# Attention and gated MLP on one core: bound on v from a sum of magnitudes on ScalarE, batch 0 scaled at its split, row-sum constants on ScalarE

## Chip, cores and metric

The kernel runs on one core of a Trainium2 chip. The metric is the device time of one execution in microseconds (us). Times of the kernel before: 1137.96 us median of three runs (1137.18 to 1144.3).

## What is computed

```python
q_d = q.reshape(B, H, Sd, factor, D).mean(axis=3)   # factor 4: 576 rows -> 144
...
out_d = sm_attn(q_d, k_d, v_d)                      # softmax attention on the means
out_up = np.repeat(out_d, factor, axis=2)
mask = np.abs(pos[:, None] - pos[None, :]) < factor # local attention: 3 neighbours each side
...
attn = attn / (np.sum(attn, axis=-1, keepdims=True) + 1e-09)
x = out_up + np.matmul(attn, v)                     # B, H, S, D = 8, 8, 576, 64 -> x is 4608 x 512
...
gate = 1.0 / (1.0 + np.exp(-(x @ w_gate)))          # 512 -> 1536
return (gate * (x @ w_val)) @ w_out                 # 1536 -> 512
```

The inputs are float32. q and k are drawn at 0.1 and then multiplied by about 6.25, w_gate by 2.946.

## The kernel before, in words

**Units and chunks.** Attention is cut into 32 units u, one for each pair of heads of a batch (four units per batch: batch b holds units 4b to 4b+3). The MLP runs over nine chunks c of 512 tokens, each in twelve pieces fc of 128 hidden columns: a gate product `pg`, a value product `pv`, and an output product `po` that adds up over fc in four PSUM banks. A large product is made of three float16 products of high and low halves, so x is split into two float16 halves (tile `xT`).

**The steps of a unit.** prep1 copies q into a block-diagonal tile (`qblk`, L438). s0 and s1 compute the local scores (`s`), add the mask (L466), take the row maximum (`mx`, L477), subtract it on GpSimd (L478) and take the exponential on ScalarE (L479). sm sums the rows (`sm`, L484), adds a tiny constant and multiplies by another (L485), takes the reciprocal (L486) and multiplies (L488). d0 and d1 do the same for the pooled scores (`sd`, maximum `mxd` L511, scaled on ScalarE L512, exponential `e` with its row sums `sme` L514); dn adds the constant (L521), takes the reciprocal (L522) and normalises into `ad` (L527 or L531). vd sums v over groups of four rows into `vdblk` (L383, L385). a0, a1 and at transpose the probabilities (`at`, `adt`) and copy them out of PSUM on ScalarE (L538), od multiplies with pooled v (`od`), and x multiplies with v (`x`), adds both (`xs`, L583 or L585) and splits the sum into `xT` (L591, L593).

**Scales.** Each batch needs a bound on |v| before its x can be scaled into float16. `vmax` (a DVE maximum of magnitudes over 128x640 for each unit, L152 into tile `vm`; four are joined at L302) gives pvb, svb = 2/pvb and sxb = 4096 svb (L305). Units 0 to 7 are "plain": v stays float32 and x is scaled by sxb while it is read out of PSUM (L567, L583). Later units scale v itself (`vsplit`, L156 and L157).

**Weights.** Each of 36 weight tiles is loaded twice: once for its maximum (`hmx`, L152), once for the conversion into float16 halves (ScalarE L205, DVE L206 to L208, ScalarE L214 and GpSimd L215; for w_out ScalarE L156 and DVE L157). This runs beside batches 0 and 1 and the first chunk.

**What sets the order.** A table T gives every step a place on one line of positions (a_* for batch 0, m_* for the others); the steps are written out in that order, and a scheduler of the library orders the instructions by it on the five in-order engines. Most v, qk, qkd and vd loads and all weight loads are issued on SP's queue. Short dummy products (`awake`) stand among batch 0's steps on TensorE. On PSUM, batch 0 uses the MLP's banks for pooled products, and all `att` tiles of the units rotate through two banks.

## Time and profile before

| | |
|---|---|
| median of the runs shown | 1137.96 us |
| profiled execution | 1139.3 us, of which the span is 1137.5 us |
| TensorE (PE) busy | 1097.7 us (96%) |
| VectorE (DVE) busy | 566.8 us (50%) |
| ScalarE (ACT) busy | 488.1 us (43%) |
| GpSimd (POOL) busy | 335.5 us (29%) |
| mean granted TensorE clock | 0.968 |

The table's shares are over the whole span. The page also cuts the span into 40 slices of 28.4 us, and the trace can be asked for any stretch, so that the opening (batches 0 and 1, the weight conversions and the first chunk) and the long rest are read apart.

### The profile page before, as it was taken

To read this page: it belongs to the slowest core of one execution; us is meant where nothing else is said; L and a number is where in the kernel's file an instruction comes from. 1 tells how busy PE (TensorE), PEld (TensorE's weight loads), DVE (VectorE), ACT (ScalarE), POOL (GpSimd) and SP (SyncE) were. 2 spreads that over 40 slices of the span, in tenths; PEclk is the share of its full clock that TensorE was granted. 3 is DMA by queue.
4 is the path that set the end of the run, shared out by engine and by line. 5 is a ranking of instruction groups with operands and counts; after the bars stand their busy time and mean duration, and the time that the engine had idled before them with its cause. 6 is when DMAs were issued, how large, how long until landed. Compare 5 with 4: busy or idle time off the path is not lost.

```text
span 1137.5 us, 16128 instructions
## 1 busy us (share of the span) xinstructions
PE 1097.7 (96%) x6319; PEld 603.6 (53%) x6319; DVE 566.8 (50%) x1048; ACT 488.1 (43%) x1112; POOL 335.5 (29%) x352
## 2 busy tenths in 40 slices
PE   7879879999999999999999999999999999999998
PEld 5854534555555555555555555555555554444443
DVE  7789989854445544444444444444444432122121
ACT  6635666533445444444445443544454332112112
POOL 6335646222223333333333332333243210000000
PEclk9758889999999999999999999999999999999999
DMA  9887766332213222132223121311121000000001
GB/s 361 330 311 258 252 210 216 118 100 86 70 47 131 60 65 70 59 111 74 69 69 106 61 65 56 119 59 54 48 94 36 1 1 37 1 1 37 1 1 37
DMA packets 31900, 110.33 MB, mean 97 GB/s; under 512 B 3536, under 2 KB 3664, under 8 KB 31824
## 3 DMA queue, kind: packets, MB, share of 16 engines
q1 hardware_dynamic: 31824, 109.30, 28.7%
q8 instruction: 50, 0.82, 0.3%
q14 instruction: 26, 0.21, 0.1%
HBM read 99.84 MB, written 9.44 MB: 96 GB/s over the span
## 4 chain that ended last, share of the span: by engine, by line
PE 86%; DVE 7%; DMA 2%; ACT 2%; issue 1%; POOL 1%; SPq 0%; DVEq 0%; ACTq 0%; POOLq 0%
PE po L394 24%; PE pg L394 23%; PE pv L394 23%; PE s L394 5%; PE x L394 3%; PE sd L394 3%; PE od L394 2%; PE at L546 1%; PE adt L556 1%; DVE wrg L207 1%; DMA v<-in_v_dram 1%; DVE vdblk L385 1%; DVE hmx L152 0%; DMA wo3c<-in_wo_dram 0%; DVE wrv L207 0%
## 5 line engine op out<-in xcount | busy, mean ns | idle before, releaser
L394 PE MATMUL pg<-xT,wg 128*128 128x512 f16 x1296 | 311.9, 383 | 6.7 <-ACT wg L214 3.5
L394 PE MATMUL pv<-xT,wv 128*128 128x512 f16 x1296 | 311.8, 381 | 0.1
L394 PE MATMUL po<-g,wo 128*128 128x512 f16 x1188 | 280.8, 379 | 0.0
L394 PEld LDWEIGHTS <-wg 128*128 128x128 f16 x1296 | 125.8, 99 | 152.0 <-issue 7.7
L394 PEld LDWEIGHTS <-wo 128*128 128x128 f16 x1296 | 124.7, 99 | 153.1 <-issue 8.2
L394 PEld LDWEIGHTS <-wv 128*128 128x128 f16 x1296 | 125.6, 99 | 141.0 <-issue 4.9
L627 DVE SCALAR_TENSOR_TENSOR tanh<-tanh,pv 128x512 f32<-128x512 f32 x108 | 73.8, 683 | 203.6 <-PE pv L394 199.3
L619 ACT ACTIVATE tanh<-pg,tsc 128x512 f32<-128x512 f32 (+7 forms) x192 | 87.0, 497 | 163.7 <-PE pg L394 163.7
L635 ACT ACTIVATE g<-tanh,gs 128x512 f16<-128x512 f32 x99 | 71.5, 723 | 149.6 <-DVE tanh L627 148.4
L636 DVE SCALAR_TENSOR_TENSOR g<-tanh,gs,g 128x512 f16<-128x512 f32 x99 | 88.6, 895 | 52.4 <-ACT g L635 51.9
L478 POOL TENSOR_TENSOR t<-t,mx 128x640 f32<-128x640 f32 x32 | 44.0, 1376 | 186.5 <-DVE mx L477 186.5
L394 PEld LDWEIGHTS s<-qk,qblk 128*128 128x128 f32 x600 | 77.9, 198 | 10.6 <-DVE hx L191 1.9
L394 PE MATMUL s<-qk,qblk 128*128 128x64 f32 x600 | 77.1, 279 | 2.6 <-DVE hx L191 1.4
L593 POOL TENSOR_TENSOR xT<-xs,xT 128x384 f16<-128x384 f32 (+7 forms) x58 | 53.1, 928 | 74.1 <-ACT xT L591 73.7
L488 POOL TENSOR_TENSOR t<-t,sm 128x640 f32<-128x640 f32 x28 | 36.8, 1316 | 96.0 <-DVE sm L486 94.6
L484 DVE TENSOR_REDUCE sm<-t 128x10 f32<-128x640 f32 x32 | 26.1, 817 | 66.1 <-ACT t L479 66.0
L156 ACT ACTIVATE vblk<-v,svb 64x640 f16<-64x640 f32 x48 | 39.7, 827 | 34.6 <-PE x L394 32.9
L466 DVE SCALAR_TENSOR_TENSOR t<-s,mk 128x384 f32<-128x384 f32 x64 | 31.0, 486 | 41.9 <-PE s L394 41.8
L438 ACT COPY qblk<-qk 64x580 f32<-64x580 f32 x60 | 40.5, 676 | 23.2 <-DMA qk<-in_qk_dram 19.5
L157 DVE SCALAR_TENSOR_TENSOR vblk<-v,svb,vblk 64x640 f16<-64x640 f32 x48 | 47.3, 985 | 3.2 <-ACT vblk L156 1.6
L512 ACT ACTIVATE mxd<-mxd 72x2 f32<-72x2 f32 x64 | 13.0, 203 | 83.5 <-DVE mxd L511 83.2
L383 POOL TENSOR_TENSOR qkd<-qkd 128x576 f32<-128x576 f32 x29 | 40.1, 1382 | 28.9 <-DMA qkd<-in_qkd_dram 28.5
(292 smaller groups left out, 1180.3 us busy)
## 6 DMA issues: line engine op xcount, KB each, us to landing
qk<-in_qk_dram SPq DMA_DIRECT2D x30, 610.0 KB, 3.8
qkd<-in_qkd_dram SPq DMA_DIRECT2D x29, 576.0 KB, 3.8
vd<-in_vd_dram SPq DMA_DIRECT2D x29, 384.0 KB, 3.5
v<-in_v_dram SPq DMA_DIRECT2D x32, 320.0 KB, 3.0
out_dram<-osb SPq DMA_DIRECT2D x16, 512.0 KB, 3.1
wo<-in_qk_dram SPq DMA_DIRECT2D x2, 610.0 KB, 10.5
wo<-in_qkd_dram SPq DMA_DIRECT2D x2, 576.0 KB, 9.3
out_dram<-osb SPq DMA_DIRECT2D x4, 256.0 KB, 2.3
```

Source lines behind the costliest of these rows:

```text
L156: nc.scalar.activation(hi, src, AF.Copy, scale=sc)
L157: nc.vector.scalar_tensor_tensor(out=lo, in0=src, scalar=sc, in1=hi, op0=ALU.mult, op1=ALU.subtract)
L383: nc.gpsimd.tensor_tensor(out=x[:, :, 0:2], in0=x[:, :, 0:2], in1=x[:, :, 2:4], op=ALU.add)
L394: nc.tensor.matmul(o, w[a], x[c], start=first and i == 0, stop=last and i == len(pairs) - 1)
L438: nc.scalar.copy(QB[ps, :, ps.start : ps.start + R], q_[ps])
L478: nc.gpsimd.tensor_tensor(out=t, in0=t, in1=mx.unsqueeze(2).to_broadcast([P, NBLK, WIN]), op=ALU.subtract)
L488: eng.tensor_tensor(out=t, in0=t, in1=sm.unsqueeze(2).to_broadcast([P, NBLK, WIN]), op=ALU.mult)
L593: eng.tensor_tensor(out=x[:, hp, 1, o : o + n], in0=src, in1=x[:, hp, 0, o : o + n], op=ALU.subtract)
L619: nc.scalar.activation(t[:, o : o + n], pt[:, o : o + n], AF.Tanh, scale=tsc[:, b, fc : fc + 1])
L627: nc.vector.scalar_tensor_tensor(out=t, in0=t, scalar=1.0, in1=pt, op0=ALU.add, op1=ALU.mult)
L635: nc.scalar.activation(g[:, 0], t, AF.Copy, scale=gs[:, fc : fc + 1])
L636: nc.vector.scalar_tensor_tensor(out=g[:, 1], in0=t, scalar=gs[:, fc : fc + 1], in1=g[:, 0], op0=ALU.mult, op1=ALU.subtract)
```

## The change

Four edits, and one number of the table T (batch 0's a_vd, the place of the pooled sums of v, goes from 1.97 to 4.6).

- `vmax` takes on ScalarE the sum of |v| over a partition's 640 values, with the accumulator of an Abs activation, in place of the DVE maximum. A sum of magnitudes is never below their maximum, so it bounds v too; the factor VUP = 512 goes into svb and out of sxb again.
- For units 0 to 3, x is read out of PSUM unscaled, and scaled by sxb in `split` (ScalarE activation with a scale, DVE multiply and subtract). Before, units 0 and 1 had their low half computed on GpSimd, units 2 and 3 on DVE; now all four have it on DVE.
- The constants of the row sums `sm` and `sme` (two tiny DVE operations for each unit) go to ScalarE.
- Batch 0's pooled sums of v are written at a later place.

```diff
-        absmax(vm[b][:, hp : hp + 1], vraw[u].rearrange("p a b -> p (a b)"))
+
+        junk = wk.tile([P, NBLK * D], F16, tag="junk", name=f"junk_{u}", bufs=1)
+        nc.scalar.activation(junk, vraw[u].rearrange("p a b -> p (a b)"), AF.Abs, accum_out=vm[b][:, hp : hp + 1])
...
-            inv_scaled(svb[:, b : b + 1], pvb[:, b : b + 1], 2.0)
-            nc.vector.tensor_scalar(out=sxb[:, b : b + 1], in0=svb[:, b : b + 1], scalar1=4096.0, scalar2=None, op0=ALU.mult)
+            inv_scaled(svb[:, b : b + 1], pvb[:, b : b + 1], 2.0 * VUP)
+            nc.vector.tensor_scalar(out=sxb[:, b : b + 1], in0=svb[:, b : b + 1], scalar1=4096.0 / VUP, scalar2=None, op0=ALU.mult)
...
-            nc.vector.tensor_scalar(out=sm, in0=sm, scalar1=EPS, scalar2=1.0 if plain else 2.0 ** -12, op0=ALU.add, op1=ALU.mult)
+            c = 1.0 if plain else VUP / 4096.0
+            nc.scalar.activation(sm, sm, AF.Copy, scale=c, bias=EPS * c)
...
-            nc.vector.tensor_scalar(out=sme, in0=sme, scalar1=EPS, scalar2=4.0, op0=ALU.add, op1=ALU.mult)
+            nc.scalar.activation(sme, sme, AF.Copy, scale=4.0, bias=EPS * 4.0)
...
-            nc.scalar.activation(od, pt[:, :SD], AF.Copy, scale=sxb[:, b : b + 1])
+            if u < NPAIR:
+                nc.scalar.copy(od, pt[:, :SD])
+            else:
+                nc.scalar.activation(od, pt[:, :SD], AF.Copy, scale=sxb[:, b : b + 1])
...
-            if plain:
+            if NPAIR <= u < NPLAIN:
...
+                if u < NPAIR:
+                    split(x[:, hp, 0, o : o + n], x[:, hp, 1, o : o + n], src, sxb[:, b : b + 1])
+                    continue
                 nc.scalar.copy(x[:, hp, 0, o : o + n], src)
```

The scheduler places instructions anew. Three places follow. In the rows a name's last number is a buffer number and the one before it the unit; the line numbers of the change are a few higher than before.

**Opening, DVE, units 0 and 1.** The first rows are those of the kernel before, from the sum of unit 0's rows.

```order
L484 TENSOR_REDUCE sm_0_200<-t_0_178 128x10
L152 TENSOR_REDUCE vm0_198<-v1_153 128x1
L466 SCALAR_TENSOR_TENSOR t_1_244<-s_1_0_237,mk_108 128x384
L485 TENSOR_SCALAR sm_0_200<-sm_0_200 128x10
L521 TENSOR_SCALAR sme_0_216<-sme_0_216 72x4
L466 SCALAR_TENSOR_TENSOR t_1_244<-s_1_3_250,mk_108 128x256
L486 RECIPROCAL sm_0_200<-sm_0_200 128x10
L522 RECIPROCAL sme_0_216<-sme_0_216 72x4
L477 TENSOR_REDUCE mx_1_256<-t_1_244 128x10
L488 TENSOR_TENSOR t_0_178<-t_0_178,sm_0_200 128x640
L511 TENSOR_REDUCE mxd_1_0_340<-sd_1_0_335 72x2
L385 TENSOR_TENSOR vdblk1_120<-wo16_111 64x3x64 x2
```

The same piece of DVE's program in the change.

```order
L487 TENSOR_REDUCE sm_0_201<-t_0_178 128x10
L469 SCALAR_TENSOR_TENSOR t_1_244<-s_1_0_237,mk_108 128x384
L469 SCALAR_TENSOR_TENSOR t_1_244<-s_1_3_250,mk_108 128x256
L480 TENSOR_REDUCE mx_1_256<-t_1_244 128x10
L515 TENSOR_REDUCE mxd_1_0_341<-sd_1_0_336 72x2
L388 TENSOR_TENSOR vdblk1_120<-wo16_111 64x3x64 x2
L490 RECIPROCAL sm_0_201<-sm_0_201 128x10
L526 RECIPROCAL sme_0_215<-sme_0_215 72x4
L515 TENSOR_REDUCE mxd_1_1_353<-sd_1_1_350 72x2
L492 TENSOR_TENSOR t_0_178<-t_0_178,sm_0_201 128x640
```

The maximum over v1 and the two constants are gone, and unit 0's reciprocals and its normalising multiply now stand behind unit 1's pooled v.

**Opening, TensorE and ScalarE, unit 3.** TensorE before, around unit 3's scores s_3 (s_3_3 are the last four blocks; x_1_8 is the end of unit 1's product with v):

```order
L125 MATMUL mxt2_488<-ident_103,hmx_131 8x128
L394 MATMUL s_3_0_521<-wo16_111,qblk1_114 128x64 x6
L394 MATMUL x_1_8_602<-at16_1_405,wg16_109 128x58 x2
L130 MATMUL mxt2_488<-mxg2_492,ones_125 128x8
L394 MATMUL s_3_3_533<-wo16_111,qblk1_114 128x64 x4
```

TensorE in the change, from behind s_3_0 on:

```order
L131 MATMUL mxt2_489<-mxg2_493,ones_125 128x8
L560 MATMUL adt_3_686<-ident_103,ad_122 128x72 x6
L397 MATMUL s_3_3_534<-wo16_111,qblk1_114 128x64 x4
L550 MATMUL at_2_0_547<-ident_103,t_2_376 128x128 x3
L397 MATMUL od_3_717<-adt16_3_693,vdblk1_120 128x144 x3
```

ScalarE in the change, up to the copy that the transposes `adt_3` wait behind and past it:

```order
L302 ACTIVATE junk_4_849,vm1_848<-v4_780 128x640
L447 COPY vblk_124<-v4_780 64x10x64 x2
L482 ACTIVATE t_2_376<-t_2_376 128x640
...
L518 ACTIVATE e_3_618,sme_3_619<-sd_3_1_632,mxd_3_1_635 72x144 x2
L572 COPY od16_2_644<-od_2_640 128x144
L447 COPY wg16_109<-v3_163 64x10x64 x2
L525 ACTIVATE sme_3_619<-sme_3_619 72x4
L157 ACTIVATE xT0_463<-xs_1_601,sxb_138 128x512
L157 ACTIVATE xT1_466<-xs_1_601,sxb_138 128x64
L531 ACTIVATE ad_122<-e_3_618,sme_3_619 72x3x48 x4
```

Unit 3's pooled transposes moved ahead of its last scores on TensorE, and what feeds them (`ad_122`) stands behind unit 3's exponentials, a copy of v3 and unit 1's split on ScalarE.

**Rest, ScalarE, unit 17.** Before:

```order
L619 ACTIVATE tanh_3_3_4794<-pg_3_3_4781,tsc_139 128x192
L619 ACTIVATE tanh_3_3_4794<-pg_3_3_4781,tsc_139 128x320
L538 CAST at16_17_4657<-at_17_0_4653 128x348
L635 ACTIVATE g_3_3_4814<-tanh_3_3_4794,gs_132 128x512
L512 ACTIVATE mxd_18_0_4695<-mxd_18_0_4695 72x2
```

In the change:

```order
L629 ACTIVATE tanh_3_3_4814<-pg_3_3_4801,tsc_139 128x192
L629 ACTIVATE tanh_3_3_4814<-pg_3_3_4801,tsc_139 128x320
L302 ACTIVATE junk_22_5210,vm5_5122<-v22_5041 128x640
L542 CAST at16_17_4677<-at_17_0_4673 128x348
L645 ACTIVATE g_3_3_4834<-tanh_3_3_4814,gs_132 128x512
```

The sum over v22 stands between a tanh and the copy of unit 17's transposes.

## Rows read from the trace of the kernel before

**Rows 1.** The page: busy tenths in 40 slices; PEclk is the granted clock.

```profile
DVE  7789989854445544444444444444444432122121
PEclk9758889999999999999999999999999999999999
```

**Rows 2.** Stretches: busy us of PE, PEld, DVE, ACT, POOL (instructions), granted clock, DMA share, GB/s.

```profile
0.00:75.00 75.00, 61.45 (x364) 51.98 (x364) 56.01 (x117) 41.00 (x108) 34.15 (x43) 0.75 0.88 333
75.00:200.00 125.00, 104.71 (x491) 53.72 (x490) 119.57 (x211) 76.35 (x152) 72.35 (x49) 0.88 0.74 242
213.00:1137.50 924.50, 919.06 (x5410) 492.03 (x5407) 378.52 (x700) 363.95 (x840) 225.86 (x257) 1.00 0.18 57
```

**Rows 3.** TensorE's waits, 0 to 200, then 230 on: total us, times, longest.

```profile
PE po L394 <- ACT wo L156: 6.0, 2, 5.1
...
PE at L546 <- DVE t L466: 0.5, 1, 0.5
PE x L394 <- DVE xs L585: 0.4, 1, 0.4
```

**Rows 4.** By line or tile: count, min/median/max ns, first and last start.

```profile
L152 DVE TENSOR_REDUCE vm<-v x32: 805/820/821, 8.8 to 775.3; 128x1 f32<-128x640 f32 x32
L485 DVE TENSOR_SCALAR sm<-sm x32: 151/170/1153, 17.7 to 902.3; 128x10 f32<-128x10 f32 x32
L479 ACT ACTIVATE t<-t x32: 721/738/753, 15.0 to 900.6; 128x640 f32<-128x640 f32 x32
L514 ACT ACTIVATE e<-sd,mxd x128: 361/368/391, 15.6 to 909.4; 72x144 f32<-72x144 f32 x128
L514 ACT ACTIVATION_READ_ACCUMULATOR e<-sd,mxd x128: 189/193/219, 15.9 to 909.7; 72x1 f32 x128
L444 ACT COPY wg<-v x8: 723/724/727, 8.9 to 53.8; 64x640 f32<-64x640 f32 x8
```

**Rows 5.** Timeline, DVE and POOL near 119: start, us, engine, line, operation.

```profile
118.95 1.52 POOL L215 TENSOR_TENSOR wv<-wrv,wv 128x512 f16<-128x512 f32 x1 [0.21 <-ACT wv L214]
119.36 1.15 DVE L485 TENSOR_SCALAR sm<-sm 128x10 f32<-128x10 f32 x1
120.42 0.41 DVE L206 TENSOR_SCALAR wrv<-wv5c 128x512 int32<-128x512 int32 x1
```

**Rows 6.** Timeline, DVE: first and last of seven constants, one's successor, another long row.

```profile
82.77 1.15 DVE L485 TENSOR_SCALAR sm<-sm 128x10 f32<-128x10 f32 x1
...
96.98 1.12 DVE L521 TENSOR_SCALAR sme<-sme 72x4 f32<-72x4 f32 x1
98.03 0.67 DVE L627 SCALAR_TENSOR_TENSOR tanh<-tanh,pv 128x512 f32<-128x512 f32 x1
...
129.01 2.59 DVE L207 SCALAR_TENSOR_TENSOR wrg<-wg6c,wrg 128x512 int32<-128x512 int32 x1
...
190.94 0.16 DVE L485 TENSOR_SCALAR sm<-sm 128x10 f32<-128x10 f32 x1
```

**Rows 7.** Chain that ended last, opening: start, us, what.

```profile
30.93 1.18 PE sd L394 x8
...
35.68 0.73 PE adt L556 x6
...
57.41 3.83 PE x L394 x20
...
63.94 0.84 DVE t L488
```

**Rows 8.** Timeline, POOL and ACT, batch 0.

```profile
55.28 1.42 POOL L593 TENSOR_TENSOR xT<-xs,xT 128x512 f16<-128x512 f32 x2 [4.13 <-ACT xT L591]
...
57.77 1.25 POOL L478 TENSOR_TENSOR t<-t,mx 128x640 f32<-128x640 f32 x1
```

**Rows 9.** Timeline, DVE and ACT near 420.

```profile
420.07 0.82 DVE L152 TENSOR_REDUCE vm<-v 128x1 f32<-128x640 f32 x1 [2.92 <-DMA v<-in_v_dram]
420.89 0.45 ACT L538 CAST at<-at 128x348 f16<-128x348 f32 x1 [1.86 <-PE at L546]
```

More of the change, by code (lines that the diff above doesn't have):

```diff
@@ L16 @@
 PSUM = bass.MemoryType.PSUM
[L20 removed]
+T = dict(ma=4.5, mas=0.45, mb=9.5, mbs=0.5, c1=56, gs=2.66, g0=16.84, r1=1.99, rs=1.6, ob=3.16, v0=15.13, v1=16.62, v2=17.5, vs=2.12, o0=18, os=1.2, pro=2.36, u4=13.82, u5=21, u6=27, u7=32, l4=1.3, l5=2.77, l6=9.47, l7=8.68, lv=15.08, vm=1.58, b8=6.75, s8=6.63, b12=26.05, s12=8.17, hold=32.07, al=0.76, am=1, z=3.68, sd=0, sn=0.79, v0m=0.61, xd=[2, 3, 7], ad=[0, 3, 7], aa=[0, 1, 2, 3, 6], td=[0, 3, 9, 10], vd=[0, 1, 2, 3, 6, 9, 10], a_prep1=-2.43, a_prep2=-0.89, a_s0=0.01, a_s1=0.52, a_sm=1.82, a_d0=2.39, a_d1=2.6, a_dn=5.17, a_a0=4.37, a_vd=4.6, a_a1=5.1, a_v=2.74, a_at=5.22, a_od=5.79, a_x=8.38, m_prep0=-3.14, m_prep1=-1.14, m_prep2=-1.43, m_s0=0.69, m_s1=2.59, m_sm=3.12, m_d0=2.84, m_d1=5.8, m_a0=10, m_dn=10.78, m_vd=11.67, m_a1=12, m_v=13.07, m_at=13.44, m_od=15.64, m_x=17, k0=30, k_prep1=4, k_prep2=0, k_s0=2, k_s1=2, k_sm=4, k_d0=3, k_d1=0, k_dn=0, k_a0=3, k_vd=8, k_a1=2, k_v=5, k_at=0, k_od=0, k_x=0)
 P = 128
@@ L48 @@
 QKSCALE = 1.0 / 8
+VUP = 512.0
 WAHEAD = 1
```

1 line of the change is left out of this document (removed).

## Prediction

> **What bounds the kernel now.** I read the slices of the page first: DVE is at 7 to 9 tenths for the first eight slices of 28.4 us and at 4 to 5 afterwards, and the granted clock is 10 tenths of full speed nearly everywhere behind them [rows 1]. So the program has an opening of some 210 us and a rest. The stretches give the two parts their bounds [rows 2]. From 213 us on TensorE is busy for 919.1 of 924.5 us at full clock, and from 230 us on the waits view has 0.9 us of waiting for it in all [rows 3]: that rest is TensorE's own work, which the change leaves as it is. From 75 to 200 us DVE is busy for 119.6 of 125 us; TensorE for 104.7 at a granted clock of 0.88, which is 2.4 GHz for part of the stretch and 1.2 GHz for the other. DVE, with the weight conversions, sets the pace there, and TensorE's largest wait, 6.0 us, is for w_out's converted halves [rows 3]. From 0 to 75 us nobody is saturated (PE 61.5, DVE 56.0, ACT 41.0 us): what counts is batch 0's chain from engine to engine, which ends in the first gate product. So the change is worth what it shortens of these two stretches, and the rest only moves earlier or later by that.
>
> **What it removes and adds.** On DVE: 32 maxima of v at 0.82 us, 0.73 from start to start, and 64 constants at 0.17 us (median), half of that from start to start, as rows overlap, where nothing holds them [rows 4]. On ScalarE instead: 32 Abs sums over 128x640, for which I take the exponential of that shape (0.74 us) plus a read of the accumulator (0.19), about 0.73 from start to start as the two overlap; and 64 tiny activations at about that read's 0.2 us [rows 4]. Batch 0's split puts two low halves more on DVE (units 0 and 1, 512 and 64 columns, about 0.74 us each) and takes as many pairs, 1.42 us each, from GpSimd [rows 8]. VUP and the scale at the split change operands only; the reading of x out of PSUM stays one DVE operation. The later place of pooled v adds no instruction and moves no load ahead of another by more than one place. SP's queue has the same transfers.
>
> **Stretch 75 to 200 us (DVE).** Seven constants fall into it, units 4 to 7, first at 82.77 and last at 190.94 us. Six of them do not take 0.16 us but 0.83 to 1.15 [rows 5, 6], and from each one's start to the next row it is 6.2 us for the seven. The reason stands in one row: the constant at 119.36 ends at 120.51, together with GpSimd's operation of 118.95 plus 1.52 = 120.47 [rows 5]. It waited for GpSimd. Is that wait removed with the operation? Other operations show it too, such as 2.59 us for a shift-and-or over 128x512, four times the 0.67 of another two-input operation of that size [rows 6]. So the wait belongs to the moment. Where the next row is such a conversion (five of the seven cases, as L206 at 120.42), it inherits the wait, and I count 0.08 us for each; where it is not (the tanh product at 98.03 reads PSUM; the reciprocal behind 82.77), the whole microsecond goes. That is 5 x 0.08 + 1.0 + 1.2 = 2.6 us. The bounds: 6.2 us if every wait goes, and 0.6 us less 0.8 us, thus a loss of 0.2, if none goes and each of four row sums now pays two hops between engines at about 0.1 us.
> The Trainium skill ("SBUF — State Buffer", section "Who interferes with whom") says that a DVE operation with two SBUF inputs, or in a two-port mode, and a GpSimd operation hold a shared port pair for the whole instruction, and the later one blocks. The trace agrees (1.15 us beside a GpSimd operation, 0.16 without one). By that rule the next two-input operation waits in place of the removed one, and this term is 2.6 us, not the 6.2 that the removed rows add up to.
>
> The maxima of batch 2 (201 us and later) lie where TensorE already has its own work in stock; I count nothing for them. What hides ScalarE's added work here is its load, 76 of 125 us [rows 2].
>
> **Opening, 0 to 75 us.** DVE loses eight maxima (5.8 us) and eight free-running constants (0.6) and gains 1.5 us of splits: 4.9 us less. But this is a chain, so I walk it. Gain: the order shows unit 3's pooled scores and unit 2's pooled transposes no longer ahead of unit 2's scores on TensorE; in the chain these are 1.18 and 0.73 us [rows 7], and batch 0's first products with v end some 2 us earlier, near 39.7 us. Loss: behind that, ScalarE's queue up to unit 3's `ad` is now, sized by rows 4 from start to start: copies of v2, v4 and v3 (two of 0.72 each, 4.4), sums over v4, v5, v6 (3 x 0.73), the exponentials of t_2 (0.64) and of unit 3 (four of 0.27 and their reads of 0.09, 1.44), `ad` itself (four of that size without the read, 1.3), and, as estimates from the same rows by size, two splits (1.3), five copies of PSUM tiles (1.6) and four tiny ones (0.4): 13.3 us [rows 4], to 53.0. TensorE's last scores of unit 3 now stand behind the transposes of `ad` (0.73) and end near 54.9; before it was 54.4. So the 2 us are used up. Then GpSimd, which before had the low half of unit 1 at 55.28 and a sum of pooled q ahead of unit 3's subtraction at 57.77 [rows 8], is free, and the subtraction can start near 56.3, 1.4 us earlier. But unit 2's product with v, which starts at 57.41 and lasts 3.83 us at a low clock, holds DVE's row sum behind it on both sides; of the 1.4 us, and with the extra hop, I keep 1.0 at the normalising multiply of 63.94 [rows 7]. From there to the first gate product the steps are the same. Taken: 1.0 us gained. Bounds: 4.9 gained, if DVE's whole saving shortens the chain; 4.3 lost, if four Abs sums (2.9) and unit 3's exponentials (1.4), now late in ScalarE's queue, all land on it.
>
> **Rest.** ScalarE now waits for v in its queue. In one unit, v22 lands at 420.07, after DVE had waited 2.92 us for it; ScalarE was idle from 419.03 to 420.89, waiting for the transposes [rows 9]. The Abs fits in with 0.73 + 0.1 us, so the copy comes at most 0.1 us later: nothing. If the cover were gone, the copy's PSUM bank is wanted again by the pooled scores about 5 us later, so some 4 us of lateness cost nothing either.
>
> **Sum.** The profiled execution took 1139.3 us (span 1137.5 and 1.8 around it): 1139.3 - 1.0 - 2.6 = 1135.7. It stood 1.3 us above the median of the runs; against that median of 1137.96 the forecast is 1134.4 us.
>
> **The rivals.**
> *All of DVE's saving counts.* For it: DVE is near saturation for most of 200 us. Against it: the waits for GpSimd are inherited, and 0 to 75 us is a chain. 4.9 + 6.2 = 11.1 us: 1127 us.
> *ScalarE's queue sets batch 0's end.* For it: unit 3's scores now stand behind `ad`. Against it: ScalarE is busy for 41 of 75 us. It decides from the point at which `ad` ends later than 53 us; at its bound 4.3 us are lost, DVE's stretch gives nothing (0.2 lost), and the result is 1142.5 us.
> *The sums over v stall the rest.* Nineteen of them stand in ScalarE's queue from v13 on. If v lands so late that the copy behind it passes the 4 us of slack, TensorE waits; at 1 us for each that is 19 us less the 3.6: 1153 us, slower. Against it: at 420 us the slack is 4 us, and DVE, which waited up to 2.9 us at these places, held nobody up. It decides from 4 us of lateness on.
> *The bound on v asks for another table on ScalarE* can be left out: the changed program's order has one table load, as before.
>
> **How the numbers follow.** Within 1% is 1126.6 to 1149.3 us, about what a measurement of this kernel can tell from no change. Forecast 0.66, with its own range 1130 to 1139; all of DVE's saving 0.17; ScalarE's queue 0.11; stalls in the rest 0.06. The first rival straddles the lower bound: with less idling TensorE may also keep 2.4 GHz longer in the opening, so 0.10 of it and 0.02 of the forecast count as faster, 0.12. Slower: the 0.06, and 0.03 for the second rival together with a clock that stays at 1.2 GHz longer: 0.09. The same: 0.79. The range of 8 in 10 reaches from 1126 to 1144 us, down to the first rival and past the second.
>
> **What would show it.** Right: from 213 us on the same TensorE waits, under 2 us; the last normalising multiply of batch 0 near 63 us; DVE still over 90% busy up to 195 us; conversions of 1 us and more at the places where constants stood. Wrong: TensorE waiting for `at` or `adt` copies behind an Abs; unit 3's last scores well behind 55 us; the rest beginning more than 6 us earlier; a granted clock of the opening far from 0.75 and 0.88.

## The result, and the profile after

The changed kernel takes 1144.77 us (median of 20 executions, 1141.03 to 1155.50) against 1139.99 us for the kernel before (20 executions, 1137.18 to 1145.87). The ratio is 1.0053, with a 95% interval of 1.0031 to 1.0074: slower by half a per cent, where a gain of 0.3% was forecast. In microseconds it lies 0.8 above the forecast range of 1126 to 1144 us; the kernel before stood 2.0 us higher in these 20 executions than in the three that the forecast started from.

The profiled execution took 1142.3 us, of which the span is 1140.5: 3.0 us more than that of before. So the trace shows a part of the loss. The other part lies between executions: of the 20, the seven below 1142.5 us had a mean granted clock of 0.970 to 0.977, the four above 1150 us one of 0.959 to 0.966. The experiments are on both parts.

First the page of the changed kernel, DVE and the granted clock in 40 slices, which answer to [rows 1], and the stretches of [rows 2] (busy us of PE, PEld, DVE, ACT, POOL, then granted clock, DMA share, GB/s):

```profile
DVE  6689989744445433444344334433444332122121
PEclk8759989999999999999999999999999999999999
```

```profile
0.00:75.00 75.00, 60.75 (x364) 51.45 (x364) 51.08 (x104) 47.43 (x132) 31.59 (x39) 0.75 0.88 329
75.00:200.00 125.00, 100.44 (x477) 49.44 (x477) 117.12 (x203) 75.23 (x154) 68.67 (x47) 0.90 0.72 242
213.00:1140.50 927.50, 919.46 (x5407) 491.25 (x5405) 348.16 (x629) 382.60 (x927) 229.44 (x259) 1.00 0.17 57
```

DVE lost 4.9 us of work in the first stretch, as was counted, and 2.5 us in the second. None of it became time: the last normalising multiply of batch 0 starts at 64.06 us (63.94 in [rows 7]), the last high half of its x on ScalarE at 73.31 (73.29), the last low half on DVE at 74.13 (73.94), and the first output of chunk 0 leaves at 235.51 (235.27). From there to the end of the span it is 905.0 us; before it was 902.2. In this execution, then, all but 0.2 us of the loss lies in the rest, which the prediction took as unchanged. TensorE's waits from 230 us on, which were two of 0.5 and 0.4 us [rows 3]:

```profile
PE sd L397 <- DVE sxb L308: 0.6, 1, 0.6
PE mxt L131 <- DVE mxg L130: 0.6, 1, 0.6
PE sd L397 <- DVE at L544: 0.4, 1, 0.4
PE at L550 <- issue: 0.3, 1, 0.3
PE x L397 <- DVE pvb L143: 0.2, 1, 0.2
PE mxt L126 <- ACT od L574: 0.2, 1, 0.2
```

All but the third and fourth belong to one moment, the bound of batch 3 at 360 us. TensorE there (timeline: start, us, engine, line, operation, in brackets the wait before it), first in the changed kernel, then before:

```profile
360.38 0.27 PE L126 MATMUL mxt<-ident,vm 128*1 128x128 f32 x1 [0.15 <-ACT od L574]
361.26 0.38 PE L131 MATMUL mxt<-mxg,ones 1*128 1x1 f32 x2 [0.61 <-DVE mxg L130]
361.88 0.97 PE L397 MATMUL x<-at,vblk 128*128 128x58 f16 x30 [0.25 <-DVE pvb L143]
363.50 0.71 PE L397 MATMUL sd<-qks 64*72 64x144 f32 x4 [0.64 <-DVE sxb L308]
```

```profile
359.35 0.27 PE L125 MATMUL mxt<-ident,vm 128*1 128x128 f32 x1
359.46 0.82 PE L394 MATMUL x<-at,vblk 128*128 128x58 f16 x24
360.31 0.38 PE L130 MATMUL mxt<-mxg,ones 1*128 1x1 f32 x2
```

Before, 24 products of x with v lie between the turning of the column of bounds and the spreading of its maximum, and cover DVE's two small steps. In the changed program the scheduler put these two rows of batch 3 next to each other, and TensorE waits out the chain: from 355 to 375 us it is idle for 1.93 us, before for 0.92. The third wait, at 724 us, is the mechanism of the rival on sums over v, seen once (timeline, all engines):

```profile
722.42 0.74 ACT L302 ACTIVATE junk<-v 128x640 f16<-128x640 f32 x1 [0.78 <-DMA v<-in_v_dram]
723.06 0.19 ACT L302 ACTIVATION_READ_ACCUMULATOR junk<-v 128x1 f32 x1
723.15 0.43 ACT L542 CAST at<-at 128x348 f16<-128x348 f32 x1
723.62 0.52 DVE L544 TENSOR_TENSOR at<-at,at 128x348 f16<-128x348 f32 x1 [1.66 <-ACT at L542]
...
724.19 0.71 PE L397 MATMUL sd<-qks 64*72 64x144 f32 x4 [0.37 <-DVE at L544]
```

ScalarE stood still for v, the transposed probabilities stood behind the sum, TensorE waited 0.37 us. Over all 32 units ScalarE was idle for 32.7 us ahead of these sums, in 21 cases (all rows that write `junk`, added up); this is the only one from 230 us on that TensorE's waits show.

### The profile page after: what moved, and what is told of

It is laid out like the page before. It is cut to its first block, busy times and chain, and to the rows that moved or that the text cites. A ratio compares the mean times of both kernels' runs of the same rounds, so it can differ in the third digit from the quotient of the medians.

```text
span 1140.5 us, 16124 instructions
## 1 busy us (share of the span) xinstructions
PE 1093.5 (96%) x6319; PEld 599.7 (53%) x6319; DVE 528.8 (46%) x956; ACT 516.9 (45%) x1240; POOL 335.9 (29%) x348
## 4 chain that ended last, share of the span: by engine, by line
PE 81%; DVE 3%; DMA 1%; ACT 1%; issue 0%; POOL 0%; DVEq 0%; POOLq 0%
PE po L397 23%; PE pg L397 23%; PE pv L397 22%; PE s L397 5%; PE sd L397 3%; PE x L397 2%; PE od L397 2%; PE at L550 1%; PE adt L560 1%; DMA qk<-in_qk_dram 1%; DMA wo7c<-in_wo_dram 0%; DVE wro L207 0%; DVE wo L158 0%; DVE wro L208 0%; DVE wrg L208 0%
## 5 line engine op out<-in xcount | busy, mean ns | idle before, releaser
L646 DVE SCALAR_TENSOR_TENSOR g<-tanh,gs,g 128x512 f16<-128x512 f32 x99 | 83.9, 847 | 59.0 <-ACT g L645 58.5
L515 DVE TENSOR_REDUCE mxd<-sd 72x2 f32<-72x288 f32 x64 | 28.8, 450 | 45.7 <-PE sd L397 45.1
```

The source lines that it names most:

```text
L646: nc.vector.scalar_tensor_tensor(out=g[:, 1], in0=t, scalar=gs[:, fc : fc + 1], in1=g[:, 0], op0=ALU.mult, op1=ALU.subtract)
```

## Experiments

Four theories were set against one another. Theory 1: the Abs sums in ScalarE's queue. Theory 2: the order of the opening, and the clock that TensorE is granted in it. Theory 3: DVE's removed work is inherited by other operations as waits for GpSimd. Theory 4: the neighbouring rows of batch 3's bound. The first expectations call theory 2 rival 2, and have a rival 3: the constants on ScalarE lengthen each unit's row sums. The table has the ratio of all executions (6 to 20 for each kernel) to those of the kernel before run beside them, and from the one profiled execution the granted clock of 44 to 60 us, the first output of chunk 0, and the time from it to the end of the span. Medians of different rounds are not to be compared: the kernel before had 1139.93 us beside the four runs no_abs to no_vd, 1139.65 beside b3_max, rest_AD, hold and drop_const, 1138.78 beside abs_open, split_vd, before_light and light, and 1139.29 beside the other four. The ratio is not the quotient of two medians either, which for no_split would be 1.0132.

| kernel | median us | ratio (95%) | clock 44:60 | chunk 0 | from there |
|---|---|---|---|---|---|
| before | 1139.99 | | 0.93 | 235.3 | 902.2 |
| changed | 1144.77 | 1.0053 (1.0031 to 1.0074) | 0.97 | 235.5 | 905.0 |
| no_abs | 1144.45 | 1.0034 (1.0014 to 1.0054) | 0.58 | 238.2 | 904.1 |
| no_const | 1149.89 | 1.0081 (1.0055 to 1.0108) | 0.50 | 243.1 | 904.6 |
| no_split | 1154.97 | 1.0107 (1.0074 to 1.0139) | 0.50 | 243.7 | 910.5 |
| no_vd | 1145.99 | 1.0046 (1.0013 to 1.0078) | 0.93 | 237.1 | 908.0 |
| b3_max | 1143.58 | 1.0023 (0.9999 to 1.0048) | 0.94 | 233.8 | 903.6 |
| rest_AD | 1139.91 | 1.0003 (0.9982 to 1.0024) | 0.50 | 241.0 | 903.4 |
| const_all | 1142.26 | 1.0026 (1.0007 to 1.0045) | 0.88 | 232.3 | 906.0 |
| const_open | 1138.79 | 1.0007 (0.9988 to 1.0026) | 0.91 | 234.9 | 902.1 |
| drop_const | 1139.32 | 0.9998 (0.9978 to 1.0018) | 0.93 | 234.8 | 902.5 |
| abs_open | 1139.84 | 1.0001 (0.9984 to 1.0019) | 0.91 | 234.6 | 902.5 |
| split_vd | 1136.91 | 0.9986 (0.9973 to 0.9998) | 0.50 | 234.6 | 902.2 |
| abc_b3 | 1147.24 | 1.0066 (1.0042 to 1.0089) | 0.63 | 244.8 | 903.7 |
| hold | 1142.63 | 1.0024 (1.0010 to 1.0038) | 1.00 | 239.6 | 903.1 |
| before_light | 1135.95 | 0.9972 (0.9959 to 0.9985) | 0.99 | 231.2 | 902.5 |
| light | 1144.70 | 1.0053 (1.0036 to 1.0070) | 0.98 | 239.8 | 902.6 |
| split_vd_light | 1143.77 | 1.0030 (1.0013 to 1.0048) | 0.80 | 239.7 | 902.3 |

The column of the clock does not tell by itself when it came back: in the profiles of split_vd and abc_b3 it was back at 33 and 38 us and fell again at 44 and 48. The last column falls into classes: 902.1 to 902.6 where the rest is as before (and for light, though it has Abs sums and constants on ScalarE there), 903.1 to 904.1 with Abs sums or constants on ScalarE in the rest and batch 3's rows apart, 904.6 to 906.0 with the rows together, and 908.0 and 910.5 with the rows together and a fallen clock behind them.

### Each of the four parts undone

no_abs (maxima on DVE again):

```diff
-VUP = 512.0
+VUP = 1.0
...
-        nc.scalar.activation(junk, vraw[u].rearrange("p a b -> p (a b)"), AF.Abs, accum_out=vm[b][:, hp : hp + 1])
+        absmax(vm[b][:, hp : hp + 1], vraw[u].rearrange("p a b -> p (a b)"))
```

> Part A undone: the bound on v is again a maximum of magnitudes on DVE; the other three parts stay. The changed kernel stands at 1.0053 of the kernel before. Theory 1 (the loss comes from the Abs sums in ScalarE's queue: v's bound, and with it the batch's scales, late in the rest, and ScalarE's queue late in the opening): about 0.995 to 1.000 of the kernel before, TensorE's waits from 230 us on back at 0.9 us, and chunk 7's first output back from 1048.1 to about 1045.4 us. Rival 2 (the loss comes from the order of the opening, and the clock that TensorE is granted there, whoever makes the bound): 1.003 to 1.006 as before. Rival 3 (the constants on ScalarE lengthen each unit's row sums): 1.003 to 1.006 too; the run without them tells it from rival 2.

no_const (constants on DVE again):

```diff
-            nc.scalar.activation(sm, sm, AF.Copy, scale=c, bias=EPS * c)
+            nc.vector.tensor_scalar(out=sm, in0=sm, scalar1=EPS, scalar2=c, op0=ALU.add, op1=ALU.mult)
...
-            nc.scalar.activation(sme, sme, AF.Copy, scale=4.0, bias=EPS * 4.0)
+            nc.vector.tensor_scalar(out=sme, in0=sme, scalar1=EPS, scalar2=4.0, op0=ALU.add, op1=ALU.mult)
```

> Part D undone: the row sums' constants are on DVE again; the other three parts stay. Theory 1 (Abs sums): 1.004 to 1.007, no better than the changed kernel. Rival 3 (the constants' hops between engines): 0.998 to 1.001, with TensorE's waits in the rest back near 1 us. If the constants on DVE only held other work's waits for GpSimd, the conversions between 74 and 225 us should go back from 106.2 to about 101 us of busy time at the same pace of the gates.

no_split (batch 0 as before):

```diff
-            if u < NPAIR:
-                nc.scalar.copy(od, pt[:, :SD])
-            else:
-                nc.scalar.activation(od, pt[:, :SD], AF.Copy, scale=sxb[:, b : b + 1])
+            nc.scalar.activation(od, pt[:, :SD], AF.Copy, scale=sxb[:, b : b + 1])
...
-            if NPAIR <= u < NPLAIN:
+            if plain:
...
-                if u < NPAIR:
-                    split(x[:, hp, 0, o : o + n], x[:, hp, 1, o : o + n], src, sxb[:, b : b + 1])
-                    continue
```

> Part B undone: batch 0's x is scaled while it is read out of PSUM again, its low halves for three of four units on GpSimd. Theory 1 (Abs sums) and rival 3 (constants): 1.004 to 1.007, as the changed kernel. If the split costs the opening (two more low halves on DVE, four scaled splits in place of copies), it comes below 1.003, with the last low half of batch 0 before 73.3 us.

no_vd (the earlier place; of the table's line only the number):

```diff
-a_vd=4.6
+a_vd=1.97
```

> Part C undone: batch 0's pooled v is summed at the earlier place. Theory 1 and rival 3: 1.004 to 1.007, as the changed kernel. Rival 2 (the order of the opening): a change of 0.3 per cent or more in either direction, with the mean granted clock of 0 to 75 us moving off 0.75.

Undoing no part brings the time back; without the split on ScalarE and DVE it is worse, and with the constants on DVE too, though there the intervals overlap. So the loss is not a sum of four prices, and each of these programs has an order of its own, so that none shows the price of one part. Theory 1's forecast for no_abs (0.995 to 1.000) fell, and so did rival 3's for no_const (0.998 to 1.001). no_split missed all that was put down for it. For no_vd rival 2 fell, which had expected a change of 0.3%: it came out as theory 1 and rival 3 had it, no different from the changed kernel. (Before the change two of batch 0's four low halves are on GpSimd, not three.) What the four profiles show instead is the clock. The changed kernel and no_split have the same TensorE rows, at the same times within 0.02 us, from 30.8 to 45 us, at 1.2 GHz in both; then one returns to 2.4 GHz and the other does not (first the stretches of the changed kernel and of no_split, then TensorE's timeline of each at 45 us):

```profile
24.00:44.00 20.00, 17.34 (x78) 15.99 (x79) 10.54 (x27) 13.23 (x45) 7.55 (x7) 0.50 0.97 387
44.00:60.00 16.00, 13.64 (x105) 11.35 (x104) 12.75 (x34) 14.81 (x44) 4.87 (x6) 0.97 0.70 234
```

```profile
24.00:44.00 20.00, 17.33 (x78) 15.98 (x79) 10.65 (x27) 13.17 (x45) 7.54 (x7) 0.50 0.97 385
44.00:60.00 16.00, 15.41 (x69) 12.20 (x68) 6.46 (x15) 11.34 (x36) 5.94 (x8) 0.50 0.50 160
```

```profile
45.23 0.71 PE L397 MATMUL sd<-qks 64*72 64x144 f32 x4
```

```profile
45.32 1.23 PE L397 MATMUL sd<-qks 64*72 64x144 f32 x4
```

Four pooled products take 0.71 us in one and 1.23 in the other. The rows are the same ahead of 30.8 us too, from 15 us on, but the clock had not fallen at the same time: five transposes, first in the changed kernel, then in no_split:

```profile
22.82 0.86 PE L560 MATMUL adt<-ident,ad 72*128 72x72 f32 x5 [0.23 <-ACT ad L531]
```

```profile
22.82 0.53 PE L560 MATMUL adt<-ident,ad 72*128 72x72 f32 x5 [0.33 <-ACT ad L531]
```

It fell between 21 and 22 us in one and between 23 and 24 in the other; whether that decides the return is not shown. In no_split the exponential of unit 3's scores starts at 67.1 us (60.6 in the changed kernel), the clock is back only near 95 us, and chunk 0 leaves 8.2 us later. (In the changed kernel it falls again at 62 us and is back at 86.) The late return is not the change's alone: the run rest_AD below, whose opening is written as before, has it too.

no_split and no_vd show a second fall, behind the waits at 360 us (stretches of no_split, then of no_vd):

```profile
355.00:375.00 20.00, 18.35 (x123) 12.00 (x121) 10.34 (x25) 11.52 (x31) 6.04 (x7) 0.91 0.30 104
375.00:395.00 20.00, 20.00 (x88) 11.14 (x88) 7.92 (x15) 9.08 (x27) 7.99 (x10) 0.75 0.33 108
```

```profile
355.00:375.00 20.00, 18.35 (x116) 12.59 (x116) 11.65 (x30) 12.11 (x34) 9.83 (x12) 0.83 0.53 176
```

A mean of 0.91 and 0.75 over two times 20 us is (0.09 + 0.25) x 20 = 6.8 us of full clock lost; 0.83 is 3.4. From chunk 1's first read of its output banks to chunk 2's it is 124.0 us in the changed kernel's profile, 129.9 and 126.8 in these: 5.9 and 2.8 us. In the changed kernel's own profiled execution, and in that of no_const with the same neighbouring rows, the clock stayed at 1.00 there.

### Batch 3's bound at 360 us

b3_max (the changed kernel, batch 3 alone with DVE's maxima):

```diff
+        up = VUP if b != 3 else 1.0
+        if b != 3:
+            junk = wk.tile([P, NBLK * D], F16, tag="junk", name=f"junk_{u}", bufs=1)
+            nc.scalar.activation(junk, vraw[u].rearrange("p a b -> p (a b)"), AF.Abs, accum_out=vm[b][:, hp : hp + 1])
+        else:
+            absmax(vm[b][:, hp : hp + 1], vraw[u].rearrange("p a b -> p (a b)"))
...
```

(Batch 3's scales then go without VUP.)

> The changed kernel with the bound of one batch only, batch 3, taken from DVE's maxima as before. In the changed program the two small TensorE operations of that batch's bound (turn the column of bounds, then spread the maximum) stand in neighbouring rows of TensorE's queue; in the kernel before 48 other rows lie between them. This edit puts 44 rows between them again and leaves all four parts as they are elsewhere. Theory 4 (TensorE waits for that chain at 360 to 366 us, 1.0 us more than before, and in some executions its granted clock falls to 1.2 GHz behind it, which costs chunk 2 another 2.8 to 5.9 us): idle time of TensorE at 355 to 375 us back under 1 us, granted clock 1.00 there, and 1.001 to 1.003 of the kernel before, median 1141 to 1143 us. Theory 1 (the Abs sums of all batches, in ScalarE's queue): 1.004 to 1.006, as the changed kernel.

The ratio is 1.0023, and with the two rows 44 apart TensorE idles for 0.20 us at 355 to 375 us in place of 1.93:

```profile
355.00:375.00 20.00, 19.80 (x132) 11.23 (x130) 12.99 (x29) 13.70 (x35) 6.54 (x9) 1.00 0.39 138
```

Its 12 executions stand in two groups, six from 1139.2 to 1140.7 us and six from 1146.4 to 1147.8; the changed kernel's are strewn from 1141 to 1155. It came out as theory 4 had it, though its interval overlaps that of the changed kernel, and it left a group some 7 us up.

const_all (the kernel before with part D alone, in all units; VUP is 1 there) has the neighbouring rows without any Abs sum.

```diff
-            nc.vector.tensor_scalar(out=sm, in0=sm, scalar1=EPS, scalar2=1.0 if plain else 2.0 ** -12, op0=ALU.add, op1=ALU.mult)
+            c = 1.0 if plain else VUP / 4096.0
+            nc.scalar.activation(sm, sm, AF.Copy, scale=c, bias=EPS * c)
...
-            nc.vector.tensor_scalar(out=sme, in0=sme, scalar1=EPS, scalar2=4.0, op0=ALU.add, op1=ALU.mult)
+            nc.scalar.activation(sme, sme, AF.Copy, scale=4.0, bias=EPS * 4.0)
```

> Part D alone, in all units: as the run above, and the constants of the rest on ScalarE too. Here the two rows of batch 3's bound stand in neighbouring places of TensorE's queue, without any Abs sum in the program. Theory 4 (this order, and not the sums, makes TensorE wait at 360 to 366 us, and behind it the clock falls in some executions): idle time of 1.5 to 2 us at 355 to 375 us, executions spread over 4 to 6 us above those of part D in the opening alone, 1.002 to 1.005. If the Abs sums are needed for that loss: no more than 1 us slower than part D in the opening alone.

Theory 4 again: 1.0026, with the same waits for DVE's mxg (0.6), pvb (0.2) and sxb (0.7), and 2.07 us of idle time in the stretch, against 0.91 and 1.0007 for const_open (the intervals overlap). The sums over v are not needed for it. This stretch explains 1.2 of the 3.9 us by which its rest is longer than const_open's; 0.8 and 0.9 us of further idle time lie near 480 and 720 us. No fall of the clock is in this profile.

rest_AD (the kernel before, Abs sums from batch 2 on, constants on ScalarE from unit 8 on; the lines of the constants are left out here):

```diff
-        absmax(vm[b][:, hp : hp + 1], vraw[u].rearrange("p a b -> p (a b)"))
+        if b >= 2:
+            junk = wk.tile([P, NBLK * D], F16, tag="junk", name=f"junk_{u}", bufs=1)
+            nc.scalar.activation(junk, vraw[u].rearrange("p a b -> p (a b)"), AF.Abs, accum_out=vm[b][:, hp : hp + 1])
+        else:
+            absmax(vm[b][:, hp : hp + 1], vraw[u].rearrange("p a b -> p (a b)"))
...
```

> The kernel before with the Abs sums for the batches from 2 on and the row sums' constants on ScalarE for the units from 8 on; the opening's work, batches 0 and 1, is as before. The two rows of batch 3's bound stand apart here. Theory 4 and theory 2 (all losses sit in the order of the opening, in one neighbouring pair of rows, and in the clock): 0.999 to 1.002, 1138 to 1142 us, with TensorE's waits from 230 us on under 1.5 us. Theory 1 (each sum costs a little wherever it stands in ScalarE's queue): 1.002 to 1.004, about 2.5 us more than before, spread over chunks 1 to 6.

The ratio is 1.0003: the sums and constants together cost the rest about a microsecond (903.4 against 902.2 in the profiles, one wait of 0.4 us for `at` among it), less than theory 1's 2.5. Its profiled execution met the late clock, with the opening's program of before: 0.50 from 44 to 60 us, unit 3's exponential at 64.7 us (59.0 before), chunk 0 at 241.0, 5.7 us later.

### Whether waits are inherited

drop_const leaves the constants of units 4 to 7 out of the kernel before (`sme` likewise):

```diff
-            nc.vector.tensor_scalar(out=sm, in0=sm, scalar1=EPS, scalar2=1.0 if plain else 2.0 ** -12, op0=ALU.add, op1=ALU.mult)
+            if not 4 <= u < 8:
+                nc.vector.tensor_scalar(out=sm, in0=sm, scalar1=EPS, scalar2=1.0 if plain else 2.0 ** -12, op0=ALU.add, op1=ALU.mult)
```

> The kernel before without the eight constants of units 4 to 7: these two tiny DVE operations for each unit are left out, so that the pooled part of these units is scaled wrongly by four. Nothing else is changed. In the profile of before the seven of them that lie between 75 and 200 us take 6.2 us from their start to the next row. If these waits for GpSimd are passed on to the next operation (the prediction's term without the ScalarE side): chunk 0 comes 0 to 2.6 us earlier, 0.998 to 1.000. If they all go: 6.2 us earlier, 0.994 to 0.996. Rival: not even the 2.6, as the conversions around take all of it.

The ratio is 0.9998, and chunk 0 is earlier by 0.4 us. The conversions took the rest. Their three operations on DVE, 36 times each between 74 and 225 us (lines L206, L207, L208; the third number is their busy time), before and then without the constants:

```profile
74.00:225.00 151.00, 20.05 (x36) 0.88 0.68 224
74.00:225.00 151.00, 32.52 (x36) 0.88 0.68 224
74.00:225.00 151.00, 27.89 (x36) 0.88 0.68 224
```

```profile
74.00:225.00 151.00, 28.57 (x36) 0.90 0.66 223
74.00:225.00 151.00, 27.21 (x36) 0.90 0.66 223
74.00:225.00 151.00, 29.98 (x36) 0.90 0.66 223
```

80.5 us became 85.8: 5.3 us more for the same work, with no other edit than that eight tiny operations are gone. The changed kernel has 24.61 + 30.25 + 30.66 = 85.5, and no_const, which puts the constants back on DVE, 21.21 + 31.71 + 28.16 = 81.1, as was expected of it. This is theory 3, and more complete than counted. One place shows it, before and then without the constants:

```profile
168.77 1.12 DVE L521 TENSOR_SCALAR sme<-sme 72x4 f32<-72x4 f32 x1
169.81 0.41 DVE L206 TENSOR_SCALAR wrv<-wv9c 128x512 int32<-128x512 int32 x1
```

```profile
167.35 1.28 DVE L206 TENSOR_SCALAR wrv<-wv9c 128x512 int32<-128x512 int32 x1
```

Before, the constant lasts until GpSimd's operation ends at 169.87 us; without it the conversion behind it lasts past the end of GpSimd's, at 168.35.

const_open (part D for units 0 to 7 alone, on the kernel before; `sme` likewise):

```diff
+            if u < 8:
+                nc.scalar.activation(sm, sm, AF.Copy, scale=c, bias=EPS * c)
+            else:
+                nc.vector.tensor_scalar(out=sm, in0=sm, scalar1=EPS, scalar2=c, op0=ALU.add, op1=ALU.mult)
```

> Part D alone and in the opening alone: the kernel before with the row sums' constants on ScalarE for the units of batches 0 and 1. The rows of batch 3's bound stand apart. Theory 3 (the wait for GpSimd is handed on): the weight conversions between 74 and 225 us, 98.3 us of busy time before, take 102 to 105 us, DVE's stretch from 75 to 200 us gives under 1 us, 0.999 to 1.001. If the constants on ScalarE alone make the clock of the opening come back late more often: a group of a third or more of the executions some 6 us above the others, 1.001 to 1.004.

Here the three lines take 81.9 us, 1.4 more than before and not the 4 to 7 that theory 3 expected, and still chunk 0 is only 0.4 us earlier. DVE now waits 1.5 us for a constant on ScalarE and 1.8 for GpSimd. So a second reason is likely beside the inherited waits: of the chain through 75 to 235 us in the kernel before, DVE carries 60 us, TensorE 53, transfers 17, ScalarE 11 and GpSimd 6, and 12 are issue (the pieces of the chain, added up). That a few microseconds taken from DVE alone do not set when it ends is argued from these shares; no run tests it by itself. Of its 12 executions four stand some 6 us up (1144.2 to 1144.6).

### The clock of the opening

abs_open (rest_AD's condition turned round, no constants moved):

```diff
-        if b >= 2:
+        if b < 2:
```

> Part A alone and in the opening alone: the kernel before with the Abs sums for the units of batches 0 and 1 on ScalarE, all else as before. The rows of batch 3's bound stand apart. If the sums in ScalarE's queue are what the opening of the changed kernel loses by: 1.002 to 1.005, batch 0's last exponential of the scores 1.5 us later (60.6 in place of 59.0) and TensorE waiting 2 us more for pooled probabilities. If the opening as a whole is a matter of when the granted clock comes back, and of nothing that this part does: 0.998 to 1.002, executions in one group near 1138 to 1141 us and a quarter of them 6 us above it, as with the kernel before.

The ratio is 1.0001, with 11 executions from 1136.1 to 1142.1, none 6 us up (3 of 29 of the kernel before beside them). No harm of part A alone in the opening shows. Unit 3's exponential did come 1.6 us later (60.7), without effect on chunk 0 (234.6).

split_vd: parts B and C alone. Its edit against the changed kernel is those of no_abs and no_const together.

> Parts B and C alone, without the Abs sums and the constants on ScalarE: batch 0's x scaled at its split, pooled v summed later. Theory 2 (an order of TensorE's rows in the opening after which the clock comes back late in more of the executions, which costs 6 to 8 us each time): the good executions stand within 1 us of before's, and more than a quarter of them stand 6 to 8 us higher; 1.000 to 1.005. If B and C save DVE or GpSimd work on batch 0's chain: batch 0's last low half earlier than 74.8 us at the same clock and 0.997 to 0.999.

The ratio is 0.9986, with 12 executions from 1134.7 to 1140.2: a gain of 0.1%, and no upper group, against theory 2's forecast. In its profile the clock is 0.76 from 24 to 44 us but 0.50 from 44 to 60, and batch 0's last low half ends late, at 77.8 us. It made that up before chunk 0 left (234.6); how is left open.

abc_b3: parts A, B and C, with batch 3's rows apart. Its edit against the changed kernel is those of no_const and b3_max together.

> Parts A, B and C together, with the constants on DVE and batch 3's maxima on DVE, so that the rows of batch 3's bound stand apart (46 rows). Part A in the opening had no execution 6 us above its group, parts B and C together had none, and all four parts had half of them there. If A, B and C together are enough (the last place of unit 3's scores on TensorE, behind the pooled probabilities): half of the executions or more near 1146 to 1148 us, median 1.003 to 1.006. If it needs the constants too: one group near 1138 to 1141 us, 0.999 to 1.002.

The ratio is 1.0066, with one of its six executions at 1141.7 and five from 1146.3 to 1150.3. What shows no harm apart makes a slow opening together, and the constants are not needed for it. In its profile this is no late return: the clock is back at 38 us, falls again at 48, and is back again only at 89.

hold: b3_max with more empty products in batch 0.

```diff
-k_d0=3, k_d1=0, k_dn=0, k_a0=3, k_vd=8, k_a1=2, k_v=5, k_at=0, k_od=0, k_x=0
+k_d0=6, k_d1=6, k_dn=0, k_a0=6, k_vd=8, k_a1=2, k_v=5, k_at=6, k_od=6, k_x=4
```

> The changed kernel with batch 3's maxima on DVE and with more of the empty products that the kernel already uses to keep TensorE busy, in the gaps of 16 to 31 us of batch 0 (26 of them for each unit in place of 8). They compute nothing. Theory 2 (the granted clock falls at 20 to 26 us because TensorE idles there, and when it comes back, at 45 us or only at 84 us, decides 6 to 8 us): the clock stays at 2.4 GHz through 44 us or comes back earlier, batch 0's last exponential of the scores comes before 58 us (60.6 in the changed kernel, 67.1 where the clock stayed low), and the time is 0.995 to 1.000 of the kernel before. If the clock follows something other than this idling: no change against the run with batch 3's maxima alone, or up to 5 us slower for the empty products that stand ahead of real ones.

The upper group is gone: 12 executions from 1139.6 to 1145.2, mean clock 0.979 to 0.986. From 24 to 44 us the clock is 0.83 in place of 0.50, which fits theory 2 (split_vd and abc_b3 reach 0.76 and 0.66 there without more empty products). But it bought no time: the empty products stand ahead of real ones, unit 3's exponential starts at 62.7, and the lower group of b3_max is 2 to 3 us better. The forecast of 0.995 to 1.000 fell.

before_light: the kernel before with 13 more for each unit, fewer than in hold.

```diff
-k_d1=0, k_dn=0, k_a0=3, k_vd=8, k_a1=2, k_v=5, k_at=0, k_od=0
+k_d1=5, k_dn=0, k_a0=3, k_vd=8, k_a1=2, k_v=5, k_at=4, k_od=4
```

> The kernel before with 13 more empty products for each unit of batch 0 (at the pooled scores, the pooled transposes and the pooled product), so that TensorE idles less from 20 to 31 us; nothing else is changed. The earlier run with 26 in place of 8 had its executions in one group from 1139.6 to 1145.2 us. Theory 2: the clock stays at 2.4 GHz or comes back before 44 us in every execution, so the group that is 6 us higher is gone; the empty products cost up to 3 us; 0.997 to 1.001, with a smaller spread. If the clock does not follow this idling: a quarter of the executions stay 6 us above the others.

The ratio is 0.9972 (0.9959 to 0.9985), with 11 executions from 1133.6 to 1138.5: better than both kernels. There is no upper group, but the kernel before had only 3 of 29 there beside it; its median moved by 2.8 us, so the gain is in most executions. Its clock from 44 to 60 and from 60 to 72 us, where the kernel before had 0.93 and 0.50 (back at 44 us in both, it falls again at 58 us before, at 72 here):

```profile
44.00:60.00 16.00, 14.76 (x124) 12.99 (x123) 12.69 (x34) 9.97 (x21) 7.17 (x8) 0.99 0.76 259
60.00:72.00 12.00, 8.79 (x69) 7.24 (x66) 11.24 (x23) 3.16 (x11) 3.51 (x7) 0.99 0.88 287
```

Batch 0's last low half ends at 70.3 us (74.8 before), and 4.1 us of it are kept at chunk 0.

light and split_vd_light carry the same three numbers (k_d1, k_at, k_od) into b3_max and into split_vd:

> The changed kernel with batch 3's maxima on DVE and 13 more empty products for each unit of batch 0 (21 in place of 8, where the earlier run had 26 to 34). Theory 2: no execution near 1147 us, as half of them were without the empty products; median 1139 to 1142 us, 1.000 to 1.002, and the empty products cost less than the 2.5 us that the larger number cost. If half of the executions stay near 1147 us, the smaller number is not enough to hold the clock.

> Parts B and C (0.9986 of the kernel before) with the 13 more empty products for each unit of batch 0 (0.9972 on the kernel before): the two things that gained, together. If they add: 0.9950 to 0.9965, 1133 to 1135 us, batch 0's last low half before 71 us. If both gain by the same thing, the return of the clock before batch 0's end: 0.997 to 0.9985, no better than the better one. If the order that B and C make meets the empty products badly, as the changed kernel did: 1.000 to 1.004.

light missed: 1.0053, six executions from 1142.1 to 1148.6. split_vd_light has 1.0030, the last of its three cases, though each of its two ingredients gained alone. In light the clock is 0.98 from 44 to 60 us and unit 3's exponential starts at 59.4, and still chunk 0 leaves at 239.8: it loses between 75 and 225 us, where TensorE waits 6.3 us for a conversion at 82.8 and 5.2 us for ScalarE at 170.8 (before, the longest waits there were 5.1 and 3.2). Gains of the opening did not add here; each program has an order of its own.

## Why the prediction was wrong, by its own steps

**The rest "only moves".** This step failed by 2.8 us in the profile; where the clock falls behind the waits, as in the profiles of no_split and no_vd, by 2.8 to 5.9 us more. It argued that TensorE's work there is unchanged and that the Abs finds room in ScalarE's queue. The second half was right in size: the sum took 0.74 us and its read 0.19, as taken from [rows 4], and with the constants and what they hold up it cost the rest about 1 us (rest_AD; 0.4 in light). The first half overlooked that the scheduler orders the rest anew too. The three programs that change the opening alone (const_open, abs_open, split_vd) keep a rest of 902.1 to 902.5 us; part D in all units brings the rows of batch 3 together (const_all), and with B and C besides it they stand apart again (no_abs). The prediction compared one unit near 420 us; the place that mattered was TensorE's pair of rows for batch 3. Theory 4's 1.4 us at full clock (905.0 against 903.6) and the ratio's step from 1.0053 to 1.0023 (whose intervals overlap) are that place.

**75 to 200 us, 2.6 us gained.** Measured: 0.2 us lost by chunk 0, the opening's 0.1 among it, and 0.4 gained where the constants are left out altogether. The failed term is the credit for whole waits. The direction of the inherited wait was right; the two whole waits that were credited (1.0 and 1.2 us) were not to be had either. The Trainium skill ("SBUF — State Buffer", section "Who interferes with whom") has the later of two operations block, where one is GpSimd's and the other a DVE operation with two SBUF inputs or in a two-port mode. The runs agree that the wait is handed on: 5.3 us more on 108 conversions. But the heirs are not only the two-input ones that the prediction named: line L206, which reads one tile, took 8.5 us more in drop_const, L208 2.1 more, and L207, which like L208 reads two, 5.3 less. Whether L206 runs in a two-port mode no run here shows.

**Opening, 1.0 us gained.** Measured: 0.1 lost at the multiply of 64.06 us. The failed steps are in the walk to unit 3. ScalarE's `ad`, put at 53.0 us, ended at 55.5. Its first and last rows (timeline of ScalarE):

```profile
42.08 1.46 ACT L447 COPY wg<-v 64x640 f32<-64x640 f32 x2 [0.34 <-PE x L397]
54.20 1.31 ACT L531 ACTIVATE ad<-e,sme 72x144 f32<-72x144 f32 x4
```

The length of the queue was sized well, 13.4 us where 13.3 were put; its start was not. Batch 0's first products with v, put at 39.7, ended at 42.0 (42.4 before): the 2 us of gain were 0.3. The pooled scores and transposes did leave their places, but the transposes of the unit before, 0.86 us, came in at 32.33 us (27.09 before), and the column of batch 0's bounds, for which TensorE waits in both, was turned at 30.76 us, 0.85 later than before. On TensorE the second half of unit 3's scores, put at 54.9, ended at 57.8. These rows show why (timeline of TensorE, then of DVE):

```profile
55.57 0.53 PE L560 MATMUL adt<-ident,ad 72*128 72x72 f32 x5 [0.18 <-ACT ad L531]
56.70 1.10 PE L397 MATMUL s<-wo,qblk 128*128 128x64 f32 x8 [0.60 <-DVE t L469]
```

```profile
55.26 0.93 DVE L158 SCALAR_TENSOR_TENSOR xT<-xs,sxb,xT 128x512 f16<-128x512 f32 x2
56.11 0.54 DVE L469 SCALAR_TENSOR_TENSOR t<-s,mk 128x384 f32<-128x384 f32 x1
```

After `adt`, the scores wait for a bank that DVE must first read, and DVE is busy with a low half that part B gave to it. GpSimd's subtraction starts at 59.28 us, where 56.3 was put and 57.77 stood before [rows 8]. That only 0.1 us of this is left at the multiply is in part luck with the clock, which fell at 62 us here and at 58 before. Unit 2's product with v took 2.44 us, where [rows 7] have 3.83:

```profile
59.73 2.44 PE L397 MATMUL x<-at,wg 128*128 128x58 f32 x20 [0.64 <-ACT at L542]
```

So DVE's row sum behind it began 0.8 us later than before (62.32 against 61.51), though the product began 2.3 later.

**The clock.** The prediction named it as a sign of error and gave it, together with the second rival, 0.03 of the slower side. In the profiled execution it was near the old values, 0.75 and 0.90. Between executions it is the largest single term, 6 to 8 us, if the upper groups are what the late clock makes; the one upper execution of these that was traced, rest_AD's, has it. The kernel before has 8 of the 35 executions beside b3_max in its upper group (mean clock 0.960 to 0.962, the others 0.967 or more), and 9, 3 and 4 of 29 in the other rounds; b3_max has 6 of 12. Half against a quarter, at 7 us, would be some 2 us of the 6.0 by which the means of the changed kernel and the kernel before differ. This is an estimate from the groups of b3_max: with 12 executions the shares are not far from what chance can do, the changed kernel's own executions form no two groups, and only one execution of each kernel was traced.

**The rivals.** That all of DVE's saving counts (1127 us) is refuted by drop_const and by chunk 0, which leaves 0.2 us later and not 11 earlier. ScalarE's queue did pass the point from which that rival was to decide (`ad` at 55.5, not 53), but cost nothing at batch 0's end. Stalls behind the sums over v occur, 0.37 us once.

**Left open:** which row of the opening makes A with B and C slow where A, and B with C, are not; what decides whether the clock comes back at 45 us; and whether the changed kernel's own executions above 1150 us have both falls of the clock. Their mean clocks (0.959 to 0.966) and no_split's profile (0.957) fit that, but no trace of one was taken.

## What to carry to other kernels

An edit to a program whose order a scheduler makes is an edit to the whole order: look, on the engine that bounds each stretch, for short dependent chains whose covering rows have gone, far from the place edited. Work taken from an engine that shares a resource with another is worth what the chain shows, not its busy time. Before counting microseconds in an opening that runs partly at 1.2 GHz, look at how the executions spread: where the clock returns and falls again may outweigh all the rest. In one order a few empty products (0.9972) gained more than four edits; in two other orders they did not (1.0053 and 1.0030).

## What the runs showed of the hardware

The same TensorE rows at the same times were followed by either clock: 2.4 GHz at 45 us in the changed kernel, 1.2 GHz until near 95 us in no_split, with chunk 0 8.2 us later. The clock had fallen about 2 us earlier in the first. A tiny DVE operation that lasts 1.12 us beside a GpSimd operation hands this wait to its successor when it is left out (1.28 us for a conversion that took 0.41). The 1.6 to 2.1 us of idling at batch 3's bound (355 to 375 us) were followed by 1.2 GHz in two of the profiles (5.9 and 2.8 us lost) and not in three others with the same waits. And more granted clock is not more speed: hold has 0.982 on average and is slower than before_light with 0.979, by 0.5% in their ratios to the kernel before.
